# Rescheduling the attention pairs of a fused attention and MoE kernel: twos from the ninth pair on, batch 2 transposed in the score banks, evictions on ScalarE, two x tiles by DMA, output tiles per engine

## The chip, the cores and the metric

One NeuronCore of a Trainium2 chip. The metric is the device time of one execution in microseconds (us), as a median over runs. "The span" is the time from the first to the last instruction in the profiled execution, some 1.7 us less than the device time. Engines in the profile: PE is TensorE, PEld its weight loads, DVE is VectorE, ACT is ScalarE, POOL is GpSimd, SP is SyncE.

A *step* in this document is one group of eight first-layer matmuls and what is emitted with it; there are 144, numbered from 0. "Steps 16 to 36" means from the start of the first matmul of step 16 to that of step 37, read from the timeline of TensorE.

## The reference

```python
# batch, heads, sequence, head size = 8, 8, 576, 64; q, k, v float32
scores = scale * q @ k.T                  # per batch and head
scores = where(|row - column| <= 32, scores, -1e9)
attn   = softmax(scores)
x      = (attn @ v) as (4608 tokens, 512)
h      = x @ w_in                         # 512 -> 2048
g      = where(h > 0, h, exp(min(h, 0)) - 1)
out    = g @ w_out                        # 2048 -> 512, float32
```

## The kernel before

A *pair* is two blocks of 64 queries, so there are 36 pairs of attention work. A tile of the MoE part has 256 tokens, so two pairs feed one tile of eight steps. Pairs *in twos* have their scores made in the same step, in two score tiles; their masks follow one step apart, and their products with V together. PSUM holds what TensorE has computed (the tiles named ps...); an *eviction* is a copy of such a result out of it, and a *cast* is a copy that changes the number format. g_sb, the activated hidden values, is made from the first layer's result ps in three instructions: e_sb (ScalarE), m_sb and g_sb (both VectorE). The attention of later pairs is woven into the MoE steps of earlier tiles by a table: `at(step, slot, function, ...)`. In the timelines below the instructions of an engine stand in the order in which they are emitted, so one that waits holds up those behind it: in step 16 of the changed kernel (its timeline stands under The result) m_sb ends at 56.55 us, the y copy behind it waits 0.31 us for TensorE, and g_sb, which reads m_sb, starts behind the copy, at 57.47.

```python
def rotate_v(b, m0, m1, parts=(0, 1)):        # V shifted by 64 keys: one VectorE copy a part
    ...
def transpose_qk(b, which, part, j0, n, evac, tag="t0"):   # n transposes on TensorE, one eviction
    ...
# pair 2..11: scores at step kk, mask (VectorE) kk+1, product with V kk+1,
#             normalize (VectorE) kk+2, x transposed by TensorE, evicted by ScalarE
FIRST_TWO = 12
begin = {4: 9, 5: 12, 6: 17, 7: 20, 8: 23, 9: 26, 10: 29, 11: 32}   # step of a pair's scores
# ... pairs 12..35 two at a time, in two score tiles "s" and "u", x transposed by DMA

def mm1(kk):                                   # first layer and the start of the ELU
    h = kk % 3 if 18 <= kk < SWAP else kk % 2  # PSUM buffer of the result
    ...                                        # 8 matmuls -> ps
    nc.scalar.activation(e_sb, ps, AX.Exp)
    nc.vector.tensor_scalar(m_sb, e_sb, -1.0, None, ALU.add)

def elu(kk):
    nc.vector.scalar_tensor_tensor(g_sb, psH.pop(kk), 0.0, m_t.pop(kk), ALU.max, ALU.min)

for kk in range(NSTEP + LAG):                  # LAG = 2
    elu(kk - 1)                                # VectorE
    run(kk, "dve")                             # masks, normalizations, V rotations
    mm1(kk)
    run(kk, "mid")                             # scores, casts, q/k transposes
    mm2(kk - LAG)                              # second layer; at a tile's end the y copies
    run(kk, "end")                             # products with V, x transposes, casts
# (cut and simplified)
```

So on VectorE the work of the slots "mid" and "end" and the y copies stand between m_sb of a step and its g_sb, and the slot "dve" stands behind the g_sb of the step before. Two things on TensorE need g_sb of a step: the second layer two steps on, and the first-layer group that takes over the same PSUM buffer, two steps on where there are two such buffers.

The softmax here doesn't subtract the row's maximum and nothing guards it: scores larger than these inputs give would overflow.

Of the kernel before, what the change touches and what calls it, by code (L numbers as in the profile page):

```python
# [9 lines left out]
FP32 = mybir.dt.float32  # L10
# [11 lines left out]
def kernel(  # L22
# [9 lines left out]
    nc = tc.nc  # L32
# [5 lines left out]
    D_MODEL = H * D  # L38
# [16 lines left out]
    STEPS = NFO // FG  # L55
# [11 lines left out]
    opool = ctx.enter_context(tc.tile_pool(name="outs", bufs=2))  # L67
# [26 lines left out]
    def ps_tile(shape, dt, tag, name):  # L94
        return pools[tag].tile(shape, dt, tag=tag, name=name)
# [16 lines left out]
    WHOLE, HALF_A, HALF_B = (0, SJ), (0, SJ // 2), (1, SJ // 2)  # L112
# [108 lines left out]
    def copy_on(eng, d_, s_):  # L221
        if eng is nc.scalar:
            nc.scalar.copy(d_, s_)  # L223
        else:
            eng.tensor_copy(d_, s_)  # L225
# [126 lines left out]
    def first_pair(b):  # L352
        return NQB * b // 2
# [77 lines left out]
    def at(kk, slot, fn, *args):  # L431
        tasks.setdefault((kk, slot), []).append((fn, args))
# [25 lines left out]
    for part, kq in ((HALF_A, 7), (HALF_B, 15)):  # L458
        for which in range(2):
            at(kq - 1 + which, "mid", cast_qk, 1, which, part, 0, SJ // 2,  # L460
               (nc.scalar, nc.vector)[which])
            at(kq + which, "mid", transpose_qk, 1, which, part, 0, SJ // 2,
               nc.vector if which and kq == 15 else nc.scalar, "s")
    for m in range(VS):
        at(13 + m // 2, "mid", load_v, 2, m)
    at(12, "dve", rotate_v, 1, 0, 2)
    at(19, "dve", rotate_v, 1, 2, VS - 1)


    FIRST_TWO = 12  # L470
    begin = {4: 9, 5: 12, 6: 17, 7: 20, 8: 23, 9: 26, 10: 29, 11: 32}
    for i in range(FIRST_TWO, NPAIR):
        begin[i] = max(STEPS * (i // 2) - 14, 37)
    for i in range(4, NPAIR):
        kk, z = begin[i], i % 2 if i >= FIRST_TWO else 0
        at(kk, "end" if i == 4 else "mid", scores, i, "u" if z else "s")
        at(kk + z, "end" if i == 4 else "mid", exponential, i)
        at(kk + 1 + z, "dve", mask, i)
        at(kk + (1 if i < FIRST_TWO else 2), "end", pv, i)
        n = kk + (2 if i < FIRST_TWO else 3 + z)  # L480
        at(n, "dve", normalize, i)
        if i < FIRST_TWO:
            at(n, "end", x_transpose, i)
            at(n, "end", x_evac, i, nc.scalar)
        else:
            at(n, "end", x_dma, i)
    SWAP = begin[FIRST_TWO] - 1
    at(SWAP, "dve", swap_back)
    starts = set(begin.values())
    starts |= {begin[i] + 1 for i in range(FIRST_TWO, NPAIR)}  # L490
    for b in range(2, B):
        k0 = begin[first_pair(b)]

        l_qk, l_v, c0 = {2: (0, 0, 16), 3: (15, 24, 21)}.get(
            b, (max(k0 - 36, 24), k0 - 22, k0 - 22))
        if b >= 3:
            at(l_qk, "mid", load_qk, b, 0, WHOLE)
            at(l_qk + 1, "mid", load_qk, b, 1, WHOLE)
            for m in range(VS):
                at(l_v + m, "mid", load_v, b, m)  # L500


        groups = [(which, j0) for which in range(2) for j0 in (0, 6, 12)]
        free = [f for f in range(c0, k0) if f not in starts]
        for n, (which, j0) in enumerate(groups):
            if b == 2:
                at(free[max(n - 1, 0)], "end", cast_qk, b, which, WHOLE, j0,
                   6, nc.vector if n < 2 or n > 3 else nc.scalar)
                at(free[n + 1], "mid", transpose_qk, b, which, WHOLE, j0,
                   6, nc.scalar)  # L510
                continue
            at(free[n], "end", cast_qk, b, which, WHOLE, j0, 6, nc.scalar)
            if j0 == 12:
                at(free[n], "end", write_rows, b, which)
                at(free[n] + 4, "mid", transpose_rows, b, which)
        for n, back in enumerate((9, 8, 5, 4) if b == 2 else (10, 8, 3, 2)):
            m0 = 2 * (n // 2)
            at(k0 - back, "dve", rotate_v, b, m0, m0 + 2, (n % 2,))



# [3 lines left out]
    psH, m_t, g_t, psY = {}, {}, {}, {}  # L525

    def mm1(kk):
        t, s = order[kk]
        h = kk % 3 if 18 <= kk < SWAP else kk % 2
        ps = ps_tile([128, FG, TT], FP32, f"h{h}", "ps")  # L530
        psH[kk] = ps
        for j in range(FG):
            fo = s * FG + j
            for do in range(NDO):
                nc.tensor.matmul(  # L535
                    ps[:, j, :],
                    lhsT=w_in_sb[:, do, fo * 128:(fo + 1) * 128],
                    rhs=xT[t][:, :, do, :],
                    start=(do == 0), stop=(do == NDO - 1))
        e_sb = mpool.tile([128, FG, TT], FP32, tag="e_sb")  # L540
        nc.scalar.activation(e_sb, ps, AX.Exp)  # L541
        m_sb = mpool.tile([128, FG, TT], BF16, tag="m_sb")
        nc.vector.tensor_scalar(m_sb, e_sb, -1.0, None, ALU.add)  # L543
        m_t[kk] = m_sb
# [7 lines left out]
    out_t = out.rearrange("(t ts p) c -> t p ts c", p=128, ts=TT // 128)  # L552

    def mm2(kk):
        t, s = order[kk]
        if s == 0:
            psY[t] = [ps_tile([128, D_MODEL], FP32, g, "psY")
                      for g in (("h2", "t0") if t == 1 else ("y0", "y1"))]
        g_sb = g_t.pop(kk)
        last = t == NT - 1 and s == STEPS - 1  # L560
        for ts in range(2):
            for j in range(FG):
                nc.tensor.matmul(  # L563
                    psY[t][ts],
                    lhsT=g_sb[:, j, ts * 128:(ts + 1) * 128],
                    rhs=w_out_sb[:, s * FG + j, :],
                    start=(s == 0 and j == 0),
                    stop=(s == STEPS - 1 and j == FG - 1))
            if last:

                y_sb = opool.tile([128, D_MODEL], FP32, tag=f"y_last{ts}",
                                  bufs=1, name="y_last")
                half = D_MODEL // 2
                nc.scalar.copy(y_sb[:, 0:half], psY[t][ts][:, 0:half])
                nc.vector.tensor_copy(y_sb[:, half:], psY[t][ts][:, half:])
                (nc.sync, nc.scalar)[ts].dma_start(out_t[t, :, ts, :], y_sb)
        if s == STEPS - 1 and not last:
            y_sb = opool.tile([128, 2, D_MODEL], FP32, tag="y_sb")
            nc.scalar.copy(y_sb[:, 0, :], psY[t][0])
            nc.vector.tensor_copy(y_sb[:, 1, :], psY[t][1])  # L580
            nc.sync.dma_start(out_t[t], y_sb)

    LAG = 2
    for kk in range(NSTEP + LAG):
        run(kk, "first")
        if 1 <= kk <= NSTEP:
            elu(kk - 1)
        run(kk, "dve")
        if kk < NSTEP:
            mm1(kk)  # L590
        run(kk, "mid")

        for n in {1: (0,), 2: (1,), 3: (2,), 4: ()}.get(
                kk, (kk - LAG,) if kk >= LAG else ()):
            mm2(n)
        run(kk, "end")
# [30 lines left out]
```

## Time and profile before

| | before |
|---|---|
| device time, median of 3 runs | 315.69 us (315.09 to 316.2) |
| span of the profiled run | 313.8 us, mean granted clock 0.998 |
| loop start (step 0) | 18.55 us |
| steps 0 to 15 / 16 to 36 / 37 to 142 | 34.58 / 50.60 / 201.45 us |
| from step 143's start to the end | 8.62 us |

The lines of the profile that carry the argument are in the prediction below. A row of a window table gives the stretch, its length, and each engine's busy us in it. "x3" behind a time is a count of instructions. In a timeline, the columns are start, duration, engine, line of the source, operation, output <- input, and in brackets the idle time of the engine just before and what ended it.

### The profile page before, as it was taken

The numbers are of one execution on the slowest core, as the hardware profiler recorded it, in microseconds if no ns is written. First come the engines' busy times: TensorE is split into PE (matmuls) and PEld (weight loads), VectorE is DVE, ScalarE is ACT, GpSimd is POOL, SyncE is SP. The second block draws the span as 40 slices with busy tenths as digits, with TensorE's granted clock in tenths as the row PEclk, the third lists the DMA queues.
The fourth block names the chain that finished last, engine by engine and source line by source line (L and its number), as shares of the span: only waits on it lengthen the run. The fifth ranks groups of instructions, "written<-read, shape, count | busy, mean of one in ns | idle before, by whom it ended". The sixth has DMA issues, their size and how long they took to land.

```text
span 313.8 us, 7504 instructions
## 1 busy us (share of the span) xinstructions
PE 295.2 (94%) x3011; PEld 197.9 (63%) x3065; DVE 247.2 (79%) x478; ACT 172.7 (55%) x262; POOL 43.0 (14%) x60
## 2 busy tenths in 40 slices
PE   6689998889999999999999999999999999999993
PEld 2456666557566676666666666666676666666661
DVE  5787687989778788888888888878888787877663
ACT  3753755677755666568356736673535353533431
POOL 8542543022011032020202000000000000000000
PEclk9999999999999999999999999999999999999999
DMA  6999999999978999979999999359111111111011
GB/s 231 191 206 271 187 155 359 372 321 132 283 166 161 316 136 202 210 105 240 307 151 148 294 296 203 112 156 185 69 36 67 36 69 34 69 36 67 0 70 67
DMA packets 90295, 52.66 MB, mean 168 GB/s; under 512 B 75156, under 2 KB 79252, under 8 KB 90260
## 3 DMA queue, kind: packets, MB, share of 16 engines
q1 hardware_dynamic: 46372, 35.92, 43.3%
q0 software_dynamic: 41728, 8.92, 43.1%
q10 hardware_dynamic: 2160, 7.34, 7.0%
q8 instruction: 24, 0.39, 0.5%
q14 instruction: 11, 0.09, 0.1%
HBM read 36.70 MB, written 15.34 MB: 166 GB/s over the span
## 4 chain that ended last, share of the span: by engine, by line
PE 80%; DVE 11%; issue 3%; ACT 3%; DMA 2%; SPq 1%; ACTq 0%; DVEq 0%
PE ps L535 37%; PE psY L563 34%; PE psS L311 3%; PE psS L279 3%; DVE g_sb L548 3%; DMA f<-in_q_dram 2%; DVE pm L299 2%; DVE x_st L323 2%; DVE m_sb L543 1%; ACT e_sb L541 1%; PE ptx L262 1%; DVE Vo L136 1%; DVE y_sb L580 1%; PE psXT L332 1%; DVE qkb L225 1%
## 5 line engine op out<-in xcount | busy, mean ns | idle before, releaser
L541 ACT ACTIVATE e_sb<-ps 128x512 f32<-128x512 f32 x144 | 86.1, 598 | 120.5 <-PE ps L535 114.9
L535 PE MATMUL ps<-xT,w_in_sb 128*128 128x256 bf16 x1152 | 149.4, 273 | 1.0 <-DVE g_sb L548 1.0
L563 PE MATMUL psY<-w_out_sb,g_sb 128*128 128x512 bf16 x524 | 139.4, 379 | 3.9 <-DVE g_sb L548 0.9
L535 PEld LDWEIGHTS <-w_in_sb 128*128 128x128 bf16 x1152 | 110.5, 98 | 38.7 <-issue 1.7
L548 DVE SCALAR_TENSOR_TENSOR g_sb<-ps,m_sb 128x512 bf16<-128x512 f32 x144 | 99.4, 690 | 13.4 <-DVE m_sb L543 0.9
L543 DVE TENSOR_SCALAR m_sb<-e_sb 128x512 bf16<-128x512 f32 x144 | 62.2, 432 | 40.0 <-ACT e_sb L541 38.1
L563 PEld LDWEIGHTS <-g_sb 128*128 128x128 bf16 x576 | 54.1, 98 | 39.5 <-DVE g_sb L548 1.8
L129 POOL DMA_DIRECT2D Ve<-in_v_dram x40 | 34.5, 868 | 132.5 <-PE psS L311 96.0
L290 ACT ACTIVATE pu<-psS 128x1024 bf16<-128x1024 f32 x36 | 36.5, 1021 | 1.5 <-PE psS L279 1.5
L223 ACT CAST qkb<-f 128x768 bf16<-128x768 f32 (+1 forms) x34 | 28.8, 848 | 0.0
L323 DVE TENSOR_TENSOR x_st<-psS,rc 128x512 bf16<-128x512 f32 x36 | 24.9, 691 | 1.3
L299 DVE TENSOR_TENSOR pm<-pu,masks 128x1024 bf16<-128x1024 bf16 x36 | 24.6, 682 | 0.6 <-ACT pu L290 0.5
L311 PEld LDWEIGHTS <-pm 128*64 128x64 bf16 x576 | 11.3, 110 | 11.7 <-DVE pm L299 8.3
L136 DVE COPY Vo<-Ve 64x1040 bf16<-64x1040 bf16 x32 | 14.6, 456 | 1.0
L311 PE MATMUL psS<-Ve,pm 128*64 128x65 bf16 x320 | 13.9, 196 | 0.7 <-DVE pm L299 0.6
L311 PE MATMUL psS<-Vo,pm 128*64 128x65 bf16 x256 | 12.4, 196 | 1.5 <-DVE Vo L136 1.0
L279 PEld LDWEIGHTS <-kT 64*128 64x128 bf16 x576 | 9.8, 95 | 6.1 <-issue 4.9
L279 PE MATMUL psS<-qT,kT 64*128 64x64 bf16 x576 | 12.2, 191 | 1.4 <-DVE kT L225 1.1
L580 DVE COPY y_sb<-psY 128x512 f32<-128x512 f32 x17 | 11.6, 683 | 0.0
L262 PE MATMUL ptx<-ident,qkb 128*128 128x128 bf16 x108 | 8.8, 220 | 2.5 <-DVE qkb L225 1.8
L262 PEld LDWEIGHTS <-qkb 128*128 128x128 bf16 x108 | 7.0, 98 | 5.3 <-DVE qkb L225 3.2
L370 PE MATMUL ps_idle<-zeros 128*128 128x512 bf16 x27 | 9.0, 470 | 1.3 <-DVE zeros L170 1.3
(33 smaller groups left out, 73.9 us busy)
## 6 DMA issues: line engine op xcount, KB each, us to landing
out_dram<-y_sb SPq DMA_DIRECT2D x17, 512.0 KB, 4.5
f<-in_q_dram SPq DMA_DIRECT2D x12, 576.0 KB, 8.9
f<-in_k_dram SPq DMA_DIRECT2D x12, 576.0 KB, 9.9
in_dram<-qkb ACTq DMA_DIRECT2D x10, 576.0 KB, 6.3
Ve<-in_v_dram POOLq DMA_DIRECT2D x24, 128.0 KB, 10.0
f<-in_q_dram SPq DMA_DIRECT2D x8, 288.0 KB, 7.3
w_in_sb<-in_moe_w_in_dram POOLq DMA_DIRECT2D x4, 512.0 KB, 15.9
w_out_sb<-in_moe_w_out_dram POOLq DMA_DIRECT2D x4, 512.0 KB, 15.9
```

Source lines behind the costliest of these rows:

```text
L129: nc.gpsimd.dma_start(out=V_e[b % 3][p0:p1, m, :, 0:D], in_=v[b, :, lo + p0:lo + p1, :].rearrange("h p d -> p h d"))
L223: nc.scalar.copy(d_, s_)
L279: nc.tensor.matmul(psS[:, h % 2, hp * 128 + z * QB:hp * 128 + (z + 1) * QB], lhsT=kT[b % 2][base:base + 64, KPAD + hp * S + QB * qb - WIN: ...
L290: nc.scalar.activation(pu, _bap(psS, [psS.ap[0], [1, 1024]]), AX.Exp, scale=SCALE)
L299: nc.vector.tensor_mul(pm, pu, _bap(mm, [mm.ap[0], [0, H], [1, 2 * QB]]))
L311: nc.tensor.matmul(psS[QB * z:QB * (z + 1), par, hp * VD:(hp + 1) * VD], lhsT=pm[:, par * HP + hp, z * QB:(z + 1) * QB], rhs=vv[:, qb // 2 ...
L323: nc.vector.tensor_mul(x_st, _bap(psS, [psS.ap[0], [VD, HP], [512, 2], [1, D]]), _bap(rc, [rc.ap[0], [2, HP], [1, 2], [0, D]]))
L535: nc.tensor.matmul(ps[:, j, :], lhsT=w_in_sb[:, do, fo * 128:(fo + 1) * 128], rhs=xT[t][:, :, do, :], start=(do == 0), stop=(do == NDO - 1))
L541: nc.scalar.activation(e_sb, ps, AX.Exp)
L543: nc.vector.tensor_scalar(m_sb, e_sb, -1.0, None, ALU.add)
L548: nc.vector.scalar_tensor_tensor(g_sb, psH.pop(kk), 0.0, m_t.pop(kk), ALU.max, ALU.min)
L563: nc.tensor.matmul(psY[t][ts], lhsT=g_sb[:, j, ts * 128:(ts + 1) * 128], rhs=w_out_sb[:, s * FG + j, :], start=(s == 0 and j == 0), stop=( ...
```

## The change

The intent is to take VectorE off the path in the first 37 steps. The diff, cut to its core:

```diff
-               nc.vector if which and kq == 15 else nc.scalar, "s")   # batch 1, keys, second half
+               nc.scalar, "s")
@@
-    FIRST_TWO = 12
-    begin = {4: 9, 5: 12, 6: 17, 7: 20, 8: 23, 9: 26, 10: 29, 11: 32}
+    FIRST_TWO, FIRST_DMA, BACK_AT = 8, 10, 18
+    begin = {4: 9, 5: 12, 6: 17, 7: 19, 8: 25, 10: 30, 12: 37}
+    # pairs from 8 on in twos; pair 7 in tile "u"; x by DMA from pair 10 on
+    # the tile "u" is there from step 18, so the third buffer of mm1 goes
@@  # batch 2: V rotations, casts, transposes
-        for n, back in enumerate((9, 8, 5, 4) if b == 2 else (10, 8, 3, 2)):   # steps 17, 18, 21, 22
+        for n, back in enumerate((3, 2, 1, 0) if b == 2 else (10, 8, 3, 2)):   # steps 22 to 25
+        if b == 2:
+            for n, (which, j0) in enumerate(((0, 0), (0, 9), (1, 0), (1, 9))):
+                at(19 + n, "mid", cast_qk, b, which, WHOLE, j0, 9, nc.vector)
+                at(20 + n, "mid", transpose_qk, b, which, WHOLE, j0, 9, nc.scalar, "s")
-        # six casts of six from step 16 on, on VectorE and ScalarE, transposes in "t0"
@@
-        h = kk % 3 if 18 <= kk < SWAP else kk % 2
+        h = kk % 2
@@  # a tile's output
-            y_sb = opool.tile([128, 2, D_MODEL], FP32, tag="y_sb")
-            nc.scalar.copy(y_sb[:, 0, :], psY[t][0])
-            nc.vector.tensor_copy(y_sb[:, 1, :], psY[t][1])
-            nc.sync.dma_start(out_t[t], y_sb)
+            for ts, eng in enumerate((nc.scalar, nc.vector)):
+                y_sb = opool.tile([128, D_MODEL], FP32, tag=f"y_sb{ts}", name="y_sb")
+                copy_on(eng, y_sb, psY[t][ts])
+                nc.sync.dma_start(out_t[t, :, ts, :], y_sb)
(cut: the last tile in the same manner, casts of batch 3, V loads of batch 2)
```

More of the change, by code (lines that the diff above doesn't have):

```diff
@@ L462 @@
             at(kq + which, "mid", transpose_qk, 1, which, part, 0, SJ // 2,
-               nc.vector if which and kq == 15 else nc.scalar, "s")
+               nc.scalar, "s")
     for m in range(VS):
-        at(13 + m // 2, "mid", load_v, 2, m)
+        at(16 + m, "mid", load_v, 2, m)
     at(12, "dve", rotate_v, 1, 0, 2)
     at(19, "dve", rotate_v, 1, 2, VS - 1)
-    FIRST_TWO = 12
-    begin = {4: 9, 5: 12, 6: 17, 7: 20, 8: 23, 9: 26, 10: 29, 11: 32}
+    FIRST_TWO, FIRST_DMA, BACK_AT = 8, 10, 18
+    begin = {4: 9, 5: 12, 6: 17, 7: 19, 8: 25, 10: 30, 12: 37}
     for i in range(FIRST_TWO, NPAIR):
-        begin[i] = max(STEPS * (i // 2) - 14, 37)
+        begin[i] = begin.get(i - i % 2, STEPS * (i // 2) - 14)
     for i in range(4, NPAIR):
-        kk, z = begin[i], i % 2 if i >= FIRST_TWO else 0
-        at(kk, "end" if i == 4 else "mid", scores, i, "u" if z else "s")
+        two = i >= FIRST_TWO
+        kk, z = begin[i], i % 2 if two else 0
+        at(kk, "end" if i == 4 else "mid", scores, i,
+           "u" if z or i == 7 else "s")
         at(kk + z, "end" if i == 4 else "mid", exponential, i)
         at(kk + 1 + z, "dve", mask, i)
-        at(kk + (1 if i < FIRST_TWO else 2), "end", pv, i)
-        n = kk + (2 if i < FIRST_TWO else 3 + z)
+        at(kk + (2 if two else 1), "end", pv, i)
+        n = kk + (3 + z if two else 2)
         at(n, "dve", normalize, i)
-        if i < FIRST_TWO:
+        if i < FIRST_DMA:
             at(n, "end", x_transpose, i)
@@ L486 @@
             at(n, "end", x_dma, i)
-    SWAP = begin[FIRST_TWO] - 1
-    at(SWAP, "dve", swap_back)
+    at(BACK_AT, "dve", swap_back)
     starts = set(begin.values())
@@ L492 @@
         k0 = begin[first_pair(b)]
-        l_qk, l_v, c0 = {2: (0, 0, 16), 3: (15, 24, 21)}.get(
+        l_qk, l_v, c0 = {2: (0, 0, 0), 3: (15, 24, 22)}.get(
             b, (max(k0 - 36, 24), k0 - 22, k0 - 22))
@@ L500 @@
                 at(l_v + m, "mid", load_v, b, m)
-        groups = [(which, j0) for which in range(2) for j0 in (0, 6, 12)]
-        free = [f for f in range(c0, k0) if f not in starts]
-        for n, (which, j0) in enumerate(groups):
-            if b == 2:
-                at(free[max(n - 1, 0)], "end", cast_qk, b, which, WHOLE, j0,
-                   6, nc.vector if n < 2 or n > 3 else nc.scalar)
-                at(free[n + 1], "mid", transpose_qk, b, which, WHOLE, j0,
-                   6, nc.scalar)
-                continue
-            at(free[n], "end", cast_qk, b, which, WHOLE, j0, 6, nc.scalar)
+        for n, back in enumerate((3, 2, 1, 0) if b == 2 else (10, 8, 3, 2)):
+            m0 = 2 * (n // 2)
+            at(k0 - back, "dve", rotate_v, b, m0, m0 + 2, (n % 2,))
+        if b == 2:
+            for n, (which, j0) in enumerate(((0, 0), (0, 9), (1, 0), (1, 9))):
+                at(19 + n, "mid", cast_qk, b, which, WHOLE, j0, 9, nc.vector)
+                at(20 + n, "mid", transpose_qk, b, which, WHOLE, j0, 9,
+                   nc.scalar, "s")
+            continue
+        free = [f for f in range(c0, k0) if f not in starts]
+        for n, (which, j0) in enumerate(
+                (which, j0) for which in range(2) for j0 in (0, 6, 12)):
+            at(free[n], "end", cast_qk, b, which, WHOLE, j0, 6,
+               nc.vector if free[n] < 24 else nc.scalar)
             if j0 == 12:
                 at(free[n], "end", write_rows, b, which)
-                at(free[n] + 4, "mid", transpose_rows, b, which)
-        for n, back in enumerate((9, 8, 5, 4) if b == 2 else (10, 8, 3, 2)):
-            m0 = 2 * (n // 2)
-            at(k0 - back, "dve", rotate_v, b, m0, m0 + 2, (n % 2,))
+                at(free[n] + (3 if free[n] == 29 else 4), "mid",
+                   transpose_rows, b, which)
     order = [(z, n) for z in range(2) for n in range(HALF)]
@@ L569, in mm2 @@
             if last:
-                y_sb = opool.tile([128, D_MODEL], FP32, tag=f"y_last{ts}",
-                                  bufs=1, name="y_last")
                 half = D_MODEL // 2
-                nc.scalar.copy(y_sb[:, 0:half], psY[t][ts][:, 0:half])
-                nc.vector.tensor_copy(y_sb[:, half:], psY[t][ts][:, half:])
-                (nc.sync, nc.scalar)[ts].dma_start(out_t[t, :, ts, :], y_sb)
-        if s == STEPS - 1 and not last:
-            y_sb = opool.tile([128, 2, D_MODEL], FP32, tag="y_sb")
-            nc.scalar.copy(y_sb[:, 0, :], psY[t][0])
-            nc.vector.tensor_copy(y_sb[:, 1, :], psY[t][1])
-            nc.sync.dma_start(out_t[t], y_sb)
+                for c, eng in enumerate((nc.scalar, nc.vector)):
+                    y_sb = opool.tile([128, half], FP32, tag=f"y_last{c}",
+                                      name="y_last")
+                    copy_on(eng, y_sb, psY[t][ts][:, c * half:(c + 1) * half])
+                    (nc.scalar, nc.sync)[c].dma_start(
+                        out_t[t, :, ts, c * half:(c + 1) * half], y_sb)
+        if s == STEPS - 1 and not last:
+            for ts, eng in enumerate((nc.scalar, nc.vector)):
+                y_sb = opool.tile([128, D_MODEL], FP32, tag=f"y_sb{ts}",
+                                  name="y_sb")
+                copy_on(eng, y_sb, psY[t][ts])
+                nc.sync.dma_start(out_t[t, :, ts, :], y_sb)
     LAG = 2
```

## The prediction

Where the text told of the hardware what no trace shows, the passage is cut and the cut marked. The forecast's sum: 44.9 + 0.6 = 45.5 us for steps 16 to 36 against 50.6, so 5.1 us gained and 315.69 - 5.1 = 310.6 us. What the traces of the kernel before show:

- TensorE's waits in the list sum to 3.0 us, the count by starts gives 6.1. The records of a first-layer group last 1.04 us, and the second-layer group behind it starts after 0.87 where nothing waits (112.10 and 112.97 us). What follows the group of step 17 (55.37 us) starts 1.21 us after it: 0.34 more than 0.87, of which the list has 0.17 as a wait.
- The kT and qT are evictions of 1152 elements: 1.35 us on VectorE, 1.12 on ScalarE.
- At the last tile VectorE's first copy waited 1.10 us, up to the end of ScalarE's copy from the same source tile.
- The 0.19 of latency: a copy that doesn't read m_sb started 0.34 us after m_sb's start (54.83 and 55.17 us), g_sb, which does, 0.53 (47.98 and 48.51).

> **What bounds the kernel now.** I read the views from coarse to fine. First the page's busy row and its forty slices:
>
> ```profile
> PE 295.2 (94%) x3011; PEld 197.9 (63%) x3065; DVE 247.2 (79%) x478; ACT 172.7 (55%) x262; POOL 43.0 (14%) x60
> ...
> PE   6689998889999999999999999999999999999993
> ...
> PEclk9999999999999999999999999999999999999999
> ```
>
> TensorE is the bound, at its full granted clock, but the early slices show 6s and 8s. I then numbered the 144 steps of the MoE loop (a step is one group of eight first-layer matmuls) by their starts in the timeline of TensorE. From step 37 on a step without attention lasts 1.74 us, 0.87 for each layer, and one with attention 2.41 to 2.48. I cut the span at step starts: loop start 18.55, step 16 at 53.13, step 19 at 61.90, step 26 at 79.33, step 37 at 103.73, last step (143) at 305.18. Busy us of each engine in those stretches:
>
> ```profile
> core 0: us, PE busy (x) PEld busy (x) DVE busy (x) ACT busy (x) POOL busy (x), PEclk, DMA share, GB/s
> ...
> 18.55:53.13 34.58, 32.43 (x351) 22.16 (x355) 26.66 (x51) 19.50 (x28) 12.22 (x16) 1.00 1.71 231
> 53.13:61.90 8.77, 7.31 (x83) 4.89 (x83) 7.75 (x15) 5.46 (x9) 0.58 (x1) 1.00 1.13 373
> 61.90:79.33 17.43, 16.24 (x191) 11.41 (x192) 14.62 (x30) 13.48 (x21) 3.65 (x4) 1.00 2.42 236
> 79.33:103.73 24.40, 22.93 (x241) 14.85 (x242) 18.72 (x38) 14.87 (x25) 2.54 (x3) 1.00 0.91 205
> 103.73:305.18 201.45, 199.40 (x2004) 136.03 (x2040) 163.46 (x314) 108.58 (x167) 10.02 (x12) 1.00 0.66 138
> ```
>
> The reader is to see that from step 37 TensorE is as good as full (199.4 of 201.45), so nothing is to be had there. In steps 16 to 18 VectorE has the larger sum. Why, the timeline of VectorE there says:
>
> ```profile
> 54.83 0.43 DVE L543 TENSOR_SCALAR m_sb<-e_sb 128x512 bf16<-128x512 f32 x1 [0.89 <-ACT e_sb L541]
> 55.17 1.35 DVE L225 COPY kT<-ptx 128x1152 bf16<-128x1152 bf16 x1
> 56.44 0.68 DVE L580 COPY y_sb<-psY 128x512 f32<-128x512 f32 x1
> 57.04 1.02 DVE L225 CAST qkb<-f 128x768 bf16<-128x768 f32 x2
> 57.97 0.68 DVE L548 SCALAR_TENSOR_TENSOR g_sb<-ps,m_sb 128x512 bf16<-128x512 f32 x1
> ```
>
> Between m_sb and its g_sb stand 2.8 us of a transposed-key eviction, an output eviction and two casts. The g_sb is what TensorE needs for the next first-layer group. TensorE's waits from 53 to 104 us:
>
> ```profile
> PE psXT L332 <- DVE x_st L323: 1.1, 2, 0.9
> PE ps L535 <- DVE g_sb L548: 0.8, 1, 0.8
> PE psS L311 <- DVE pm L299: 0.6, 1, 0.6
> PE ptx L262 <- DVE y_sb L580: 0.5, 1, 0.5
> ```
>
> All are for VectorE. They understate the loss[...]. So I count TensorE's work instead, by start-to-start times in its timeline: a bare step 1.735; one pair's scores 0.34, its probabilities times V 0.37, its x transposes 0.22; nine q/k transposes 0.50, six 0.33. Steps 16 to 36 before hold 21 x 1.735 + 6 x (0.34 + 0.37 + 0.22) + 0.50 + 6 x 0.33 = 44.5 us and take 103.73 - 53.13 = 50.6. **About 6.1 us are waits; that is the prize.** Steps 0 to 15 lose some 3 us in the same sense, but the change leaves their order alone.
>
> [...] The trace has 1.35 (VectorE, kT) and 1.12 (ScalarE, qT)[...]
>
> **The change, part by part.** Costs are start-to-start on VectorE: m_sb followed by g_sb 1.14 a step; mask 0.61; reciprocal and normalize 0.84; V rotation 0.43; y copy 0.60; cast of nine 0.67, of six 0.51. An operation between m_sb and g_sb hides the 0.19 of latency between them.
>
> 1. Eviction of batch 1's second key half to ScalarE: VectorE loses 1.27 in step 16, ScalarE gains about 1.03; it is busy there only 5.46 of 8.77.
> 2. Batch 2: six casts, transposes and evictions in steps 16 to 25 become four of nine in 19 to 23. The casts cost VectorE 4 x 0.67; evictions are all on ScalarE. On TensorE 36 transposes either way. What matters is that no cast stands in steps 16 and 17 any more, where the two output copies fall.
> 3. Pairs 8, 9 and 10, 11 as twos: the same instructions, but a pair's mask has a step of slack before its product and normalization, as later in the steady phase. The third buffer for the first layer's result goes, so step n+2 now waits for g_sb of step n.
> 4. x of pairs 10 and 11 by DMA: 2 x 0.22 off TensorE, two 0.6 evictions off ScalarE.
> 5. y tiles per engine: takes no busy time away; it doubles the output DMAs.
>
> Sums by group of steps in the changed order, VectorE / TensorE:
> - 16 to 18: 5.2 / 6.4 (pair 6, two y copies, nine transposes).
> - 19 to 23: 12.6 / 11.8. Step 19 alone is 3.3 on VectorE: two V rotations, the normalization of pair 6, a cast.
> - 24 to 29: 12.0 / 12.3.
> - 30 to 36: 12.3 / 13.6.
>
> The larger of each pair sums to 6.4 + 12.6 + 12.3 + 13.6 = 44.9 us. Laying the first ones end to end by hand, in the order of the instructions, gives step 19 at 59.65 in place of 61.90, a TensorE wait of 0.4 for pair 6's x there, and no wait over 0.1 in 20 to 25. I add 0.6 for small hand-over waits (the pairs 7, 8 and 9 still have their x transposed on TensorE behind a normalization; step 33 carries a normalization and a y copy). 45.5 against 50.6 is **5.1 us gained by step 37**. From there the cadence is the same: 0. The tail: [...] ScalarE now issues a DMA between its two copies (about 0.36 more before the second) and the last transfer is half as large, 128 KB: 0, give or take 0.4. So 315.69 - 5.1 = 310.6.
>
> **The rivals.**
> - *VectorE becomes the bound of steps 19 to 25.* For: its sum passes TensorE's in 19 to 23, and one late g_sb now stops the next group but one. Against: the steady phase runs on two such buffers too, with up to 2.28 us of VectorE work in a step of 2.42, and shows only two small waits (0.1 and 0.2 us) in 106 steps. It would give back 2 to 3 us: 313.
> - *The DMAs become the wait.* For: the q/k loads and V loads of batches 2 and 3 land in a crowded stretch (4.63 as DMA share near 72 us; V landings of 27 us between 40 and 70), the first cast of batch 3 now stands on VectorE, in front of g_sb, and an x of pair 10 or 11 queues behind a key transpose on SP. Against: loads issued at 43 to 51 us land in 10 to 13, the casts come at 62 or later; x of pair 11 is issued near step 36 and needed at 40. It would make 312 to 315.
> - *Only the first-wait part counts, the grouping nothing.* Steps 26 to 36 before hold 21.9 us of work by the same count and take 24.4. If twos don't remove that 2.5, the gain is 2.6 to 3: 312.8.
> - *All waits of 16 to 36 go and the tail shortens by half a us:* 50.6 - 44.1 = 6.5, so 309 or a little less.
>
> **Range and chances.** The faster-by-2% line is 309.4, beyond my sum by 1.2, and near the most that the order allows. I give it 0.22; slower by 2% would need a new DMA wait of 11 us: 0.02. The range runs from all waits removed to half of the gain lost.
>
> **What would show it.** Right: step 16 starts near 53.1 as before, step 19 near 59.6, step 37 near 98.5; steps 17 and 18 at 2.1 to 2.3 in place of 3.3; no VectorE operation over 0.7 between m_sb and g_sb in steps 16 and 17; steps 37 to 142 unchanged at about 201.5. Wrong: steps 19 to 23 above 13 us with TensorE waiting for g_sb or x_st (first rival); a VectorE cast or V rotation ended by a DMA (second); steps 26 to 36 still above 23.5 us (third); a span after step 143 that differs from 8.6 by over 0.5 (the tail).

## The result

311.87 us (311.07 to 312.94, 6 runs) against 315.76 us for the kernel before in the same rounds. The ratio is 0.9877, 95% interval 0.985 to 0.9904; a ratio is the mean time of one kernel's fast runs over that of the other's fast runs of the same rounds, so not quite the quotient of the medians. Six more runs later, beside the last experiment, gave 311.64 us and 0.9861.

The changed kernel's busy us by the same stretches, cut at its own step starts (loop start, steps 16, 19, 26, 37, 143):

```profile
0.00:20.30 20.30, 15.60 (x137) 8.16 (x138) 11.81 (x31) 9.40 (x13) 14.28 (x26) 0.83 1.46 211
20.30:54.42 34.12, 32.78 (x356) 22.15 (x355) 26.54 (x51) 19.50 (x28) 13.00 (x15) 1.00 1.82 228
54.42:61.37 6.95, 6.71 (x78) 4.47 (x77) 5.50 (x10) 5.15 (x8) 0.00 (x0) 1.00 1.12 372
61.37:78.06 16.69, 16.42 (x198) 11.52 (x194) 15.67 (x31) 12.08 (x16) 2.94 (x3) 1.00 1.86 268
78.06:101.22 23.16, 22.36 (x237) 14.73 (x236) 19.97 (x41) 13.94 (x23) 3.31 (x4) 1.00 1.21 196
101.22:302.43 201.21, 201.21 (x2042) 135.89 (x2040) 163.50 (x314) 108.61 (x167) 10.04 (x12) 1.00 0.71 143
302.43:310.90 8.47, 3.80 (x21) 1.78 (x19) 3.05 (x6) 1.34 (x3) 0.00 (x0) 0.92 0.19 63
```

The reader is to compare lengths. The stretch of steps 16 to 18 went from 8.77 to 6.95 us, 19 to 25 from 17.43 to 16.69, 26 to 36 from 24.40 to 23.16. Together that is 50.60 to 46.80: **3.80 us**, essentially the whole gain. From step 37 on nothing moved (201.45 and 201.21), nor did the end (8.62 and 8.47). The loop of this execution happened to start 1.75 us later, at a clock of 0.83 in the first row; that is no part of the change, and the section on the spread of runs comes back to it.

In steps 16 and 17 VectorE now does only a y copy between m_sb and g_sb (changed kernel, timeline of VectorE; step 16, step 17 is alike):

```profile
56.12 0.43 DVE L548 TENSOR_SCALAR m_sb<-e_sb 128x512 bf16<-128x512 f32 x1 [0.57 <-ACT e_sb L546]
56.86 0.69 DVE L225 COPY y_sb<-psY 128x512 f32<-128x512 f32 x1 [0.31 <-PE psY L568]
57.47 0.68 DVE L553 SCALAR_TENSOR_TENSOR g_sb<-ps,m_sb 128x512 bf16<-128x512 f32 x1
```

VectorE even waits for TensorE ahead of the copy; step 17 lasts 2.18 us in place of 3.34.

But 46.80 us is 2.7 more than TensorE's 44.1 us of work in those steps. Its waits in the changed kernel from 54 to 102 us, in the order engine, output, releaser, total, times, longest:

```profile
PE ps L540 <- DVE g_sb L553: 0.6, 1, 0.6
PE psXT L332 <- DVE x_st L323: 0.5, 2, 0.3
PE psS L311 <- DVE pm L299: 0.2, 1, 0.2
```

The first is in step 35. VectorE ahead of it, and TensorE's line that waits:

```profile
95.60 0.68 DVE L225 COPY y_sb<-psY 128x512 f32<-128x512 f32 x1
96.20 0.68 DVE L553 SCALAR_TENSOR_TENSOR g_sb<-ps,m_sb 128x512 bf16<-128x512 f32 x1
96.80 0.20 DVE L320 RECIPROCAL rc<-psS 128x8 f32<-128x8 f32 x1
97.03 0.69 DVE L323 TENSOR_TENSOR x_st<-psS,rc 128x512 bf16<-128x512 f32 x1
97.76 0.43 DVE L136 COPY Vo<-Ve 64x1040 bf16<-64x1040 bf16 x1
98.22 0.43 DVE L548 TENSOR_SCALAR m_sb<-e_sb 128x512 bf16<-128x512 f32 x1
98.75 0.69 DVE L553 SCALAR_TENSOR_TENSOR g_sb<-ps,m_sb 128x512 bf16<-128x512 f32 x1
...
99.49 0.38 PE L540 MATMUL ps<-xT,w_in_sb 128*128 128x256 bf16 x2 [0.56 <-DVE g_sb L553]
```

Step 33's y copy, step 34's normalization and its V rotation follow each other without a gap; g_sb of step 34 ends at 99.44, and the first-layer group of step 36, which takes over its buffer, starts at 99.49. Counted by step length over its work, the remaining waits are 0.72 us in step 35, 0.56 in 19, 0.43 in 18, 0.38 in 28, 0.24 in 32 and some tenths elsewhere. In step 18 the product of pair 6 waits for its mask (0.2 us in the list above), which VectorE starts only after the second y copy and g_sb of step 17.

### The profile page after: what moved, and what is told of

The parts are those of the page before. It is cut to its first block, busy times and chain, and to the rows that moved or that the text cites. A ratio compares the mean times of both kernels' runs of the same rounds, so it can differ in the third digit from the quotient of the medians.

```text
span 310.9 us, 7573 instructions
## 1 busy us (share of the span) xinstructions
PE 298.9 (96%) x3057; PEld 198.7 (64%) x3057; DVE 246.1 (79%) x479; ACT 170.0 (55%) x255; POOL 43.6 (14%) x60
## 4 chain that ended last, share of the span: by engine, by line
PE 82%; DVE 8%; DMA 4%; issue 2%; ACT 2%; POOL 1%; SPq 0%; ACTq 0%; DVEq 0%
PE ps L540 36%; PE psY L568 35%; PE psS L311 3%; PE psS L279 3%; DMA Ve<-in_v_dram 3%; DVE g_sb L553 3%; PE ptx L262 2%; DMA f<-in_q_dram 2%; PE ps_idle L370 2%; DVE m_sb L548 1%; DVE x_st L323 1%; ACT e_sb L546 1%; DVE Vo L136 1%; DVE pm L299 1%; DVE y_sb L225 1%
## 5 line engine op out<-in xcount | busy, mean ns | idle before, releaser
L568 PE MATMUL psY<-w_out_sb,g_sb 128*128 128x512 bf16 x576 | 147.9, 379 | 1.0 <-DVE g_sb L553 1.0
L223 ACT CAST qkb<-f 128x768 bf16<-128x768 f32 (+1 forms) x30 | 25.4, 848 | 0.0
L279 PE MATMUL psS<-qT,kT 64*128 64x64 bf16 x576 | 12.3, 193 | 0.9 <-DVE kT L225 0.9
L370 PE MATMUL ps_idle<-zeros 128*128 128x512 bf16 x29 | 11.0, 533 | 1.3 <-DVE zeros L170 1.3
L225 DVE CAST qkb<-f 128x1152 bf16<-128x1152 f32 (+3 forms) x16 | 9.8, 640 | 2.6 <-DMA f<-in_q_dram 2.6
```

The source lines that it names most:

```text
L223: nc.scalar.copy(d_, s_)
L279: nc.tensor.matmul(psS[:, h % 2, hp * 128 + z * QB:hp * 128 + (z + 1) * QB], lhsT=kT[b % 2][base:base + 64, KPAD + hp * S + QB * qb - WIN: ...
L568: nc.tensor.matmul(psY[t][ts], lhsT=g_sb[:, j, ts * 128:(ts + 1) * 128], rhs=w_out_sb[:, s * FG + j, :], start=(s == 0 and j == 0), stop=( ...
```

## The experiments

All twelve gave correct results. The table has, for each kernel, the median time and the step lengths, from the starts in its own trace. The times come from five sets of rounds, not all on one chip; the kernel before took 315.76 us beside the changed kernel, 315.83 beside e1 to e4, 316.32 beside e5 and f1 to f3, 316.37 beside g1 and g2, and 315.71 beside g3 and h1.

| kernel | us | steps 16 to 18 | 19 to 23 | 24 to 29 | 30 to 36 | 16 to 36 |
|---|---|---|---|---|---|---|
| before | 315.76 | 8.77 | 12.57 | 14.24 | 15.02 | 50.60 |
| e2: before, key eviction moved | 315.22 | 7.90 | 12.79 | 14.23 | 15.02 | 49.94 |
| g1: e2 and V rotations moved | 312.95 | 7.33 | 11.99 | 14.25 | 15.02 | 48.59 |
| **changed** | 311.87 | 6.95 | 12.53 | 12.79 | 14.53 | 46.80 |
| e1: changed, key eviction back | 312.16 | 7.20 | 12.53 | 12.78 | 14.53 | 47.04 |
| e3: changed, pairs 8 to 11 single | 312.69 | 6.95 | 12.53 | 13.87 | 14.07 | 47.42 |
| e4: changed, one output tile | 311.55 | 6.95 | 12.54 | 12.79 | 14.52 | 46.80 |
| e5: changed, x of 10, 11 by TensorE | 311.60 | 6.96 | 12.53 | 12.78 | 14.79 | 47.06 |
| f1: changed, batch 3 rotations moved | 311.66 | 6.95 | 12.53 | 12.54 | 14.51 | 46.53 |
| f2: changed, batch 1 rotations moved | 312.26 | 6.95 | 12.27 | 12.78 | 14.53 | 46.53 |
| f3: changed, more fillers | 311.69 | 6.95 | 12.75 | 12.79 | 14.52 | 47.01 |
| g2: both, and a row write later | 310.55 | 6.95 | 12.20 | 12.55 | 13.71 | 45.41 |
| g3: g2 and more fillers | 309.99 | 6.95 | 12.14 | 12.54 | 13.71 | 45.34 |
| h1: changed, again | 311.64 | 6.95 | 12.53 | 12.79 | 14.52 | 46.79 |

Times of a few runs each differ by up to 1.5 us for what happens before the loop, so the last column is the better judge of one part. f3 and h1 show its own noise: the same work from step 16 on takes 46.79 to 47.01 us. (In e3 the first pair starts one step earlier, so 24 to 29 and 30 to 36 are to be taken together: 27.94 against 27.32.)

**1. The key eviction put back on VectorE.**

```diff
-               nc.scalar, "s")
+               nc.vector if which and kq == 15 else nc.scalar, "s")
```

> The changed kernel with one line undone: batch 1's second key half is again evicted by VectorE (step 16). My theory (work put between m_sb and g_sb on VectorE holds back the next first-layer group): step 17's start to step 18's start grows from 2.18 us to 3.0 or more, step 37 starts 0.9 to 1.3 us later after the loop's start than the 80.92 us of the changed kernel, so about 313.0 us. Rival (ScalarE, which now evicts it, was as much on the path, or the grouping of pairs alone brings the gain): within 0.3 us of the changed kernel. [...]

Step 17 grew from 2.18 to 2.43 us only, and steps 16 to 36 by 0.24; timed, 312.16 us. (From the loop's start, the mark that the expectation names, step 37 comes 1.73 us later, 82.65 against 80.92; but 1.49 of these lie in steps 0 to 15, which the edit leaves alone, and the changed kernel's second profile has 82.36 there.) My theory as I had put it, in which each us ahead of g_sb is paid, missed; the rival's bound held. VectorE had slack there. Timeline of VectorE in this kernel:

```profile
55.47 0.43 DVE L548 TENSOR_SCALAR m_sb<-e_sb 128x512 bf16<-128x512 f32 x1 [0.89 <-ACT e_sb L546]
55.81 1.35 DVE L225 COPY kT<-ptx 128x1152 bf16<-128x1152 bf16 x1
57.08 0.68 DVE L225 COPY y_sb<-psY 128x512 f32<-128x512 f32 x1
57.67 0.68 DVE L553 SCALAR_TENSOR_TENSOR g_sb<-ps,m_sb 128x512 bf16<-128x512 f32 x1
```

g_sb follows m_sb by 2.2 us, not by the 3.14 of the kernel before. A part of the 1.35 us copy, 0.31, fills the time in which the y copy had waited for TensorE in the changed kernel. g_sb ends 4.59 us after step 16's start in place of 3.73; but step 18, which needs it, starts 4.42 us after it in the changed kernel, so most of the 0.86 us is slack, and 0.25 reaches TensorE.

**2. The key eviction alone moved in the kernel before.**

```diff
-               nc.vector if which and kq == 15 else nc.scalar, "s")
+               nc.scalar, "s")
```

> The kernel before with only the eviction of that key half moved to ScalarE. My theory: of the two casts, the y copy and the eviction that stood between m_sb and g_sb in step 16 only 1.27 us go; step 17 shrinks from 3.34 us to 2.2 to 2.6, and the whole gains 0.7 to 1.2 us: about 314.8. Rival (the six-column casts in steps 16 and 17 are what counts): step 17 stays at 3.0 or more and the time within 0.3 us of before.

Step 17 fell from 3.34 to 2.48 us, as my theory had it; step 18 stayed at 3.19 and step 19 gave 0.21 back (3.56), so 0.66 us are left by step 37. The timed runs (315.22 us, ratio 0.9975, 0.994 to 1.001) can't tell that from nothing. Experiments 1 and 2 make a square for step 17: with casts and eviction ahead of g_sb 3.34, without the eviction 2.48, without the casts 2.43, without both 2.18. (The corners without the casts have the rest of the change too. The V rotations at least don't disturb it: experiment 9 moves them and has 2.48 as well.) **Either removal takes most of the loss; the second then has little left to take.** So the eviction is worth 0.66 us in one kernel and 0.24 in the other, and its share of the gain can't be given as one number.

**3. Pairs 8 to 11 one at a time in the changed kernel.**

```diff
-    FIRST_TWO, FIRST_DMA, BACK_AT = 8, 10, 18
-    begin = {..., 7: 19, 8: 25, 10: 30, 12: 37}
+    FIRST_TWO, FIRST_DMA, BACK_AT = 12, 10, 18
+    begin = {..., 7: 19, 8: 24, 9: 26, 10: 29, 11: 32, 12: 37}
-           "u" if z or i == 7 else "s")
+           "u" if z or i in (7, 9, 11) else "s")
(and batch 3's casts and batch 2's rotations held at the changed kernel's steps)
```

> The changed kernel with pairs 8 to 11 one at a time (starts at steps 24, 26, 29, 32, banks s and u in turn, product one step and normalization two steps after the scores), all else as changed; batch 3's casts and V rotations at the same steps. My theory (twos leave a step of slack between mask, product and normalization): steps 24 to 36 take 1.5 to 2.5 us longer than the 27.32 us (73.90 to 101.22) of the changed kernel. Rival (the grouping brings nothing, the gain is the new home of batch 2's casts and evictions): within 0.5 us.

Steps 24 to 36 took 27.94 us against 27.32: the twos are worth 0.62 us, not 1.5 to 2.5. Both theories missed, each on its side. (A first version in one score tile deadlocked when it was built; by my reading pair 9's scores stood ahead of pair 8's transposed x in the same tile.) These singles use two score tiles in turn, where the kernel before had one, so what the second tile gives is in both of the compared kernels.

**4. The output tile shared again.** The diff's last hunk undone.

> The changed kernel with the output tiles of before (one tile for both engines, one DMA of 512 KB). My theory: no busy time and no wait of TensorE hangs on it: from loop start to step 143 within 0.3 us of the changed kernel's 282.13, and the tail after step 143's start 8.6 us against 8.5. Rival (the shared tile held VectorE up behind ScalarE, as the last tile seems to show): 0.5 us or more slower, with small waits coming back in steps 63 and 92, which were there before and are gone in the changed kernel.

Steps 16 to 36 46.80 us, as changed; the end 309.7 - 301.11 = 8.59 us. Steps 63 and 92 lasted 1.74 and 2.47 us as in the changed kernel, and also in experiment 2, which has the old tile: the small waits of the first profile were chance. The output tiles count for nothing. At the end of the changed kernel's trace the waits are still there:

```profile
306.06 0.37 ACT L223 COPY y_last<-psY 128x256 f32<-128x256 f32 x1 [1.96 <-PE psY L568]
306.46 0.36 ACTq L581 DMA_DIRECT2D out_dram<-y_last  x1
306.46 0.42 DVE L225 COPY y_last<-psY 128x256 f32<-128x256 f32 x1 [1.10 <-ACT y_last L223]
306.86 0.37 ACT L223 COPY y_last<-psY 128x256 f32<-128x256 f32 x1 [0.43 <-PE psY L568]
...
307.26 0.42 DVE L225 COPY y_last<-psY 128x256 f32<-128x256 f32 x1 [0.38 <-ACT y_last L223]
```

VectorE's copies still wait for ScalarE's, though they write other tiles now. What they still share is the source tile in PSUM; that this is the cause was not tested by itself. And ScalarE's DMA issue stands between its two copies.

**5. x of pairs 10 and 11 by TensorE.**

```diff
-    FIRST_TWO, FIRST_DMA, BACK_AT = 8, 10, 18
+    FIRST_TWO, FIRST_DMA, BACK_AT = 8, 12, 18
```

> The changed kernel with x of pairs 10 and 11 again transposed by TensorE and evicted by ScalarE. My theory: TensorE gets 2 x 0.22 us more work in steps 33 and 34, each behind a normalization that VectorE ends late, and a y copy in step 33: steps 30 to 36 grow from 14.53 us by 0.6 to 1.2. Rival (that stretch is set by VectorE, whose work is the same, so the transposes hide in its waits): 0.3 us or less.

Steps 30 to 36 grew by 0.26 us: the rival. Steps 33, 34 and 35 lasted 1.97, 2.50 and 1.73 us in place of 1.74, 1.74 and 2.46, so by step lengths some 0.2 of the 0.44 us of transposes lie in time in which TensorE would have waited in step 35.

**6. Batch 3's V rotations moved.**

```diff
-        for n, back in enumerate((3, 2, 1, 0) if b == 2 else (10, 8, 3, 2)):
+        for n, back in enumerate({2: (3, 2, 1, 0), 3: (7, 6, 1, 0)}.get(b, (10, 8, 3, 2))):
```

> The changed kernel with batch 3's four V rotations in steps 30, 31, 36, 37 in place of 27, 29, 34, 35. My theory of what is left over: in steps 34 and 35 the y copy, two normalizations and a rotation follow one another on VectorE, g_sb of step 34 comes 0.7 us late and the next group but one, which has only two buffers, waits for it (step 35 lasts 2.46 us where 1.74 is bare); likewise the rotation of step 27 delays x of pair 8 (step 28 2.34, work 1.96). Moved, step 35 falls to 1.74 to 1.85, step 28 by 0.1 to 0.3, and step 37 starts 0.7 to 1.1 us earlier after step 16. Rival (the late g_sb is from the y copy and the normalizations alone): step 35 keeps 0.4 us or more of its wait.

Steps 28 and 35 fell about as expected, to 1.97 and 1.88 us. But step 32 rose from 2.71 to 3.27, so only 0.27 us are left of the 0.7 to 1.1 that I had expected. The rotation in step 31 had met a mask (timeline of VectorE in this kernel):

```profile
89.01 0.68 DVE L299 TENSOR_TENSOR pm<-pu,masks 128x1024 bf16<-128x1024 bf16 x1
89.72 0.43 DVE L136 COPY Vo<-Ve 64x1040 bf16<-64x1040 bf16 x1
90.18 0.43 DVE L549 TENSOR_SCALAR m_sb<-e_sb 128x512 bf16<-128x512 f32 x1
90.72 0.69 DVE L554 SCALAR_TENSOR_TENSOR g_sb<-ps,m_sb 128x512 bf16<-128x512 f32 x1
91.32 0.68 DVE L299 TENSOR_TENSOR pm<-pu,masks 128x1024 bf16<-128x1024 bf16 x1
```

There is no gap in these lines, and the second mask is what pair 11's product waits for.

**7. Batch 1's last V rotations moved.**

```diff
-    at(19, "dve", rotate_v, 1, 2, VS - 1)
+    at(16, "dve", rotate_v, 1, 2, VS - 1)
```

> The changed kernel with batch 1's last two V rotations in step 16 in place of 19. My theory: step 19 falls from 2.86 us to 2.3 to 2.45 (its work on TensorE is 2.3), step 17 gains 0.0 to 0.3 since VectorE idles 0.57 us before m_sb of step 16; net 0.3 to 0.5 us less from step 16 to 24. Rival (total VectorE work of steps 16 to 23 is the bound and placement within it counts for nothing): within 0.1 us.

Step 19 fell from 2.86 to 2.42 us and steps 16 to 18 did not grow (6.95): the place counts, not the total. Step 23 was 0.18 longer in this trace, so 0.27 us are left, a little under what I had expected; it was 0.22 longer in experiment 8 too, which changes nothing there, so I don't put that down to the move; what made it longer is not shown here.

**8. More fillers at the start.**

```diff
-    idle(10, "y1")
+    idle(13, "y1")
```

> The changed kernel with 13 in place of 10 filler matmuls at the very start. My theory of the spread between runs (loop start at 18.2 us in some profiles, 20.1 to 20.3 in two): where the first q load lands late, TensorE stands still for 1.6 us or more near 6 us and the granted clock falls to 0.50 for some 6 us; three more fillers of 0.44 us bridge that. Then no profile shows a clock below 0.9 between 8 and 16 us, the runs lie within 0.8 us of each other, and the median falls 0.3 to 0.8 us to about 311.2. Rival (the late load itself sets the loop start, the clock only goes with it): the spread of 1.5 us and more stays.

The four runs had clocks of 0.996 to 0.999, none fell; but they spread over 1.2 us (310.85 to 312.04), more than I had expected, and the median is 311.69, not 311.2. Experiment 7's profile meanwhile showed the clock falling at 16 us, where in the changed kernel's it fell near 9: 1.00 from 15 to 16 us, 0.53 in the next us, 0.50 in the two after. So my account of *what* opens the gap was too narrow.

**9. Two lines of the change in the kernel before.**

```diff
-               nc.vector if which and kq == 15 else nc.scalar, "s")
+               nc.scalar, "s")
-        for n, back in enumerate((9, 8, 5, 4) if b == 2 else (10, 8, 3, 2)):
+        for n, back in enumerate((4, 3, 2, 1) if b == 2 else (10, 8, 3, 2)):
```

> The kernel before with two lines of the change: the key half evicted by ScalarE, and batch 2's four V rotations in steps 22 to 25 in place of 17, 18, 21, 22. The casts stay in steps 16 to 22, in six pieces, with one pair at a time. My theory (steps 17 to 19 are long for whatever stands ahead of g_sb there; evictions, casts and rotations use the same slack): steps 16 to 18 fall from 7.90 us with the eviction alone to 7.0 to 7.3, step 19 from 3.56 to 3.0 or less; steps 22 to 25 gain up to 0.5; step 37 at 82.8 to 83.6 us after the loop's start, against 84.57 with the eviction alone. Rival (the casts of batch 2 alone hold steps 17 to 19): 16 to 18 stay at 7.7 or more.

Steps 16 to 18 7.33 us, step 19 2.77, and step 37 starts 82.81 us after the loop's start: my theory, if only just (0.41 of the last figure's gain lies in steps 0 to 15). 50.60 - 48.59 = 2.0 of the 3.8 us come with two edits, the rotations giving 1.35 of them; 312.95 us, ratio 0.9888 (0.9852 to 0.9925). By the timed ratios alone this can't be told from the whole change (0.9877); the step lengths tell them apart. Steps 22 to 25 gained nothing in length from the four rotations that came to stand there.

**10. Other places for what holds g_sb back.** Experiments 6 and 7 together, with both early rotations of batch 3 in step 30, where VectorE idled 1.22 us in experiment 6 even with one, and ScalarE's last row write one step later:

```diff
+        ... 3: (7, 7, 1, 0) ...
+    at(16, "dve", rotate_v, 1, 2, VS - 1)
-                at(free[n], "end", write_rows, b, which)
+                at(free[n] + (free[n] == 29), "end", write_rows, b, which)
```

> The changed kernel with other places for what holds g_sb back: batch 3's V rotations two in step 30, one each in 36 and 37; batch 1's last two in step 16; batch 3's last row write issued by ScalarE one step later, after e_sb and the exponential of step 30. My theory: the rotation of step 31 in the last try cost 0.6 us because a mask is on the path there, while VectorE idles 1.2 us in step 30 behind ScalarE's cast and DMA issue. Then step 19 at 2.42, 28 at 1.97, 32 at 2.5 to 2.75, 35 at 1.74 to 1.9; steps 16 to 36 take 45.2 to 45.7 us against 46.80, and the run 1.1 to 1.6 us less than the changed kernel: about 310.4. Rival (VectorE's total in 30 to 36 is the bound and the wait only moves): steps 30 to 36 stay within 0.2 us of 14.53.

Step 19 2.41, step 28 1.97, step 32 2.47, step 35 1.87; steps 30 to 36 13.71; steps 16 to 36 45.41 us, all as expected but step 32, which fell 0.03 under its range, and 310.55 us. Three things were moved together here; what each gives in steps 30 to 36 was not measured.

**11 and 12. The same with fillers, and the changed kernel beside it.**

```diff
-    idle(10, "y1")
+    idle(13, "y1")
     front_transpose(1, HALF_B, nc.scalar, ("y0", "y1"))
+    idle(4, "h0")
```

> The last version (other places for rotations and row write) with fillers at the start: 13 in place of 10 at the very start, and 4 more after the second key half's transposes (near 14 us), where TensorE stands still for a microsecond and more. My theory: runs with a mean granted clock near 0.985 are those in which the clock fell to 0.50 before the loop, and each costs 0.7 to 1.7 us; with both gaps filled no run has a clock under 0.99, the loop starts by 18.6 us, and the median falls by 0.2 to 0.6 us below the 310.55 of the same kernel without fillers. Rival (the gaps have nothing to do with the clock): about a quarter to a half of the runs still show 0.985 to 0.99.

> The changed kernel itself, on the same chip and in the same rounds as the version with other places and fillers. All theories: 311.0 to 313.0 us, some of its runs with a clock near 0.985, and 1.2 to 2.0 us slower than that version.

309.99 us against 311.64 us. The means of the six runs of each in the same rounds are 310.27 and 311.62: 1.36 us, ratio 0.9956. **This is the lowest median of all kernels here**, at 0.9818 of the kernel before (0.9785 to 0.9851); that the fillers add to experiment 10 (0.9824, 0.9778 to 0.9869) is not shown. Five of its six runs lie between 309.97 and 310.32; in the sixth (311.35, the profiled one) the loop waited for a load of w_in until 19.54 us, against the 18.6 that I had expected. Nor did any of the changed kernel's six runs show a clock near 0.985 this time, as I had expected some to.

*The spread of runs.* In the changed kernel's first profile VectorE waited 2.57 us, until 7.12, for the first q load (1.35 us, until 5.90, in the kernel before's), TensorE stood still for 1.96 us, up to 7.67 us, and the granted clock, 1.00 from 8 to 9 us, was 0.58 in the next us and 0.50 after. Two stretches of that execution, then of the later one of the same kernel (third column from the right is the clock):

```profile
8.00:12.00 4.00, 2.96 (x51) 2.15 (x49) 2.56 (x6) 2.65 (x4) 2.39 (x3) 0.64 2.11 214
12.00:16.00 4.00, 4.00 (x17) 2.02 (x16) 3.02 (x6) 2.73 (x4) 2.23 (x3) 0.50 2.54 155
```

```profile
8.00:12.00 4.00, 2.90 (x56) 1.97 (x56) 2.62 (x6) 3.16 (x5) 2.23 (x3) 1.00 2.16 217
12.00:16.00 4.00, 3.31 (x52) 1.92 (x51) 3.33 (x9) 2.45 (x4) 2.70 (x4) 1.00 2.55 161
```

The loops of these two start at 20.30 and 17.83 us. Mean clocks below 0.99 came in 11 of the 48 runs of kernels with the old fillers (kernel before not counted) and in none of the 10 with more. At that rate none in 10 has a chance of (37/48)^10 = 7%; with the 32 runs of the kernel before in the experiments' rounds, 5 of them below 0.99, it is (64/80)^10 = 11%. So that the fillers prevent it is possible and not shown. What goes with a lower mean clock looks clear within experiment 5: 310.93 and 311.09 us at clock 1.000, 312.11 and 312.29 at 0.985 and 0.989. But in experiment 10 the slowest run (311.32) had 0.999. And a mean clock above 0.99 does not rule out a slow start: experiment 7's profile, listed at 0.993, has the fall to 0.50 told of above, and its loop started at 19.66 us. (At 0.50 the 32 score matmuls near 10.8 us took 1.04 us in the changed kernel's first profile, against 0.64 at 1.00 in the kernel before.)

## Why the prediction was right

It gave 310.6 us, most likely within 2% of the kernel before. The first six runs gave 311.87, the later six 311.64. The gain is 3.9 to 4.1 us in place of 5.1: the mechanism and the place were right, and one term was too small.

- *What bounds the kernel, and where the prize lies.* Right. Steps 0 to 15 (34.58 and 34.12, which differ by more between runs of one kernel), 37 to 142 and the end did not move.
- *Steps 16 to 18: 6.4 us, 19 to 23: 12.6.* Measured 6.95 and 12.53. The first misses step 18's 0.43 us, pair 6's mask behind a y copy; in the second VectorE's sum of 12.6 was the right bound, as VectorE had but one wait there, of 0.3 us.
- *Steps 24 to 29: 12.3, 30 to 36: 13.6.* Measured 12.79 and 14.53. Here the hand count was too kind.
- *The mis-sized term* is "0.6 for small hand-over waits". Against the 44.9 us of the group sums the stretch took 1.9 us more, not 0.6 (0.55 in the first group, -0.07, 0.49 and 0.93 in the others). Against TensorE's work of 44.1 us the prediction left room for 1.4 in all (45.5); it is 2.7. I had named step 33's normalization and y copy as carrying a small wait, but not that step 34's normalization and V rotation add to them; that alone is 0.72 us in step 35. Experiment 10 removed 1.4 us of these waits by places alone and came to 45.41 us.
- *The signs.* Step 18 lasted 2.53 us, not 2.1 to 2.3; from step 16's start, step 19 came at 6.95 us, not 6.5, and step 37 at 46.80, not 45.4. The other signs of being right came (step 16 at 54.42 us and not 53.1 only by the late start of that execution; 53.40 in the later one), and none of being wrong. One reading was incomplete: TensorE's waits before are not all for VectorE; the list also has 0.3 us for an x eviction on ScalarE.
- *The parts.* "What matters is that no cast stands in steps 16 and 17": supported by experiment 1, where the eviction stands there alone and steps 16 to 18 take 7.20 against 8.77 us; but casts and V rotations were moved together there. The prediction did not list the move of batch 2's V rotations out of steps 17 and 18 as a part, and experiment 9 shows that it gives 1.35 us. The eviction's 1.27 us of VectorE time were worth 0.24 to 0.66. The twos are worth 0.62; the x transposes by DMA 0.26 of their 0.44; the output tiles nothing, as foretold.
- *First rival, VectorE as the bound of 19 to 25.* VectorE was the bound of 19 to 23, but no more than the sums had it: this did not cost 2 to 3 us. Its mechanism, a late g_sb that stops the group two steps on, did appear, in step 35. Whether the removed third buffer would have absorbed it was not tried: the second score tile takes its room.
- *Second rival, the DMAs.* Not seen: from 54 to 102 us no wait of VectorE or TensorE in the changed kernel is ended by a DMA.
- *Third rival, grouping brings nothing.* Half right: steps 26 to 36 went from 24.40 to 23.16 us where all of the 2.5 had been hoped for, and twos as such give 0.62.
- *Fourth, all waits go and the end shortens.* Not so.

What stays open: how the remaining 0.9 us or so of the 3.8, which no single undoing shows and the two edits of experiment 9 don't give either (3.8 - 2.0 - 0.62 - 0.26 = 0.9), divide between the casts in fours, their new steps, and the transposes in the score tile. The parts share slack, so the sum is itself only rough.

## What to carry to other kernels

On an engine that works in order, look at what stands between an instruction and the one that the bottleneck waits for, and count it by place and not by total: moving four copies of 0.43 us to steps that they did not lengthen gave 1.35 us here, taking 1.27 us off VectorE where it had slack only 0.24 to 0.66. Two parts of a change that relieve the same wait don't add up, so undo one *and* do one alone before giving either its share. And take differences from marks inside the trace when what happens before them varies by more than the effect.

## What else the traces show

- While GpSimd issues V loads (four back to back in experiment 1, 3.42 us, so some 0.86 each), two V rotations take 0.74 and 0.87 us in place of 0.43, and an m_sb 0.84 in place of 0.43. The m_sb ends at 47.31 us, GpSimd's stretch at 47.84. Others that overlap such an issue keep their 0.43 (one rotation at 46.3 us in the changed kernel), so when it happens is open, and that the issue causes it was not tested. Step 13 took between 2.36 us (changed kernel, where one rotation was lengthened, to 0.79) and 3.16 (experiment 1, with the two rotations and the m_sb); that is as much as several parts of this change. Experiment 1, GpSimd then VectorE:

```profile
44.42 3.42 POOL L129 DMA_DIRECT2D Ve<-in_v_dram  x4 [1.11 <-DMA Ve<-in_v_dram]
44.79 1.64 DVE L136 COPY Vo<-Ve 64x1040 bf16<-64x1040 bf16 x2
46.47 0.84 DVE L548 TENSOR_SCALAR m_sb<-e_sb 128x512 bf16<-128x512 f32 x1
```

- The granted clock was at 0.50 for some 6.8 us in the changed kernel's first profile, from about 1.5 us after a gap of TensorE of 1.96 us; in experiment 7 it was at about 0.50 for some 3.4 us, from near 16 us, and TensorE's longest gap from 13 us to there was 0.96. In the changed kernel's later profile a gap of 1.18 us, up to 6.46 us, left it at 1.00. So the length of the gap before it alone does not decide.
- A row write landed 6.9 us after its issue, as a median of the ten in the changed kernel, but the issue took 0.55 to 0.63 us of ScalarE's in-order time, once just ahead of e_sb of step 30 (0.59 us at 88.24, e_sb at 88.93). Experiment 10 moved that one away, together with two rotations, and step 32 fell from 2.71 to 2.47 us; the share of the write alone was not measured.
